# A chunked state-space scan ahead of a gated FFN: the prologue rebuilt around an earlier pair 0

## The chip, the cores and the metric

One core of a Trainium2 chip. The metric is device time of one execution in microseconds (us), the median of the runs. The engines are TensorE (PE; its weight loads are listed apart as PEld), VectorE (DVE), ScalarE (ACT), GpSimd (POOL) and SyncE (SP), which only starts DMAs here.

## The reference

Two parts. First a scan over 768 tokens for 4 batches and 8 heads, in chunks, with head size D = 32 and state size N = 16; then an FFN over all 3072 tokens with 256 features (8 heads x 32).

```python
for c in range(nc):                      # chunks along the sequence
    cum = cumsum(log(a))                 # inside the chunk
    L = exp(cum[i] - cum[j]) * causal
    y_intra = (C @ B.T * L) @ x
    y_inter = C @ state * exp(cum)
    state = exp(sum(la)) * state + (B * exp(cum[-1] - cum)).T @ x
    y[chunk] = y_intra + y_inter
gate = maximum(y @ w_gate, 0)            # y as (3072, 256); w_gate, w_val: 256 x 1536
out = (gate * (y @ w_val)) @ w_out       # w_out: 1536 x 256
```

The result does not depend on the chunk length, and the kernel takes 128 tokens. It also replaces exp(cum[i] - cum[j]) by a product of two factors: with P the running product of a, C is multiplied by P[i] and one of the other factors is divided by P[j].

## The kernel before, in words

**Units.** A *pair* p is 256 tokens of one batch, two chunks of 128 (12 pairs, 3 to a batch). A *block* is 512 tokens, two pairs, the unit of the FFN (6 blocks). In block b the FFN works on pairs 2b and 2b+1 while the scan prepares pairs P = 2b+2 and Q = 2b+3 in between. The scan of pairs 0 and 1 is the prologue. `in_order` (L15) ties every engine to the order of the program, so the order in the code is the order on each engine.

**A pair's steps.** `load` brings x, B and C. `scale_bc` (L253) makes bs in bf16: B divided and C multiplied by the decay P. `cast_x` (L275) casts x. `transp` (L307) turns B and C with TensorE into PSUM, `tevac` (L320) copies them out as BT and, masked for two groups of four heads, as CT. `G` (L355) computes B C^T for all heads into four PSUM banks, `gevac` (L373) copies them to gs and applies the causal mask (ScalarE with POOL for two banks, VectorE with a mask for two). `Dm` (L429) multiplies gs with x into y. `astep` (L393) adds B^T x to the running state in A_ps, `sevac` copies it masked to Sm, `inter` (L417) adds Sm C to y, and `yevac` (L443) copies y to yT, which the FFN reads.

**Wide pairs.** Pairs 0 to 3 (NWIDE = 4) are loaded with two neighbouring tokens on one partition, so that one DMA run is 128 bytes for B and C and 256 for x. Their tokens are therefore not in order on the partitions. `sort_wide` (L286) brings B and x into token order with eight matmuls per pair against a permutation (`order`, L153) and copies the result to bx.

**Decay.** One scan on VectorE gives cp, the running products of each half sequence (L194). Small fp32 matmuls with `pick` bring the wanted heads to the token's partition: `wide_decay` (L201) for a wide pair and `decay` (L227) for all the others, both followed by reciprocals and copies.

**FFN.** `gvh` (L469) is one slice f of 128 hidden units for half a block (256 tokens): four matmuls into one bank, relu on ScalarE to r, product on VectorE to h. `gv` (L455) is the same for 512 tokens and two banks. `fout` (L485) multiplies h with w_out, `foevac` stores the result. A block is four slices as halves (first for pair 2b, then for 2b+1), eight whole ones, then four parts of output, with the scan of P and Q in between.

**Buffers.** PSUM has five shared banks (`bank`, L66) in rotation, for G, gate, val, o and the like, and one each for tp, y and A_ps.

**Start.** `keep_warm` issues matmuls on zeros: 8, then 4 behind the decay matmuls, then 7 after pair 0's G. The weights come in three parts of four slices, and w_out in one, all issued by POOL. `wait_for` (L185) holds POOL's issue of a part until a certain load has landed. The loads of pairs 2 and later are issued by SyncE; B of pair 2 and all that follows it there wait for a memset on VectorE (L81).

Of the kernel before, what the change touches and what calls it, by code (L numbers as in the profile page):

```python
# [29 lines left out]
def kernel(  # L30
# [40 lines left out]

# [3 lines left out]
    def wide_bc(p, qb, qc):  # L75
        b, c0 = p // PPB, 2 * (p % PPB)
        sl = slice(c0 * 128, (c0 + 2) * 128)
        bcr = raw.tile([128, NH, 2, 2, N], FP32, tag="bcr", name="bcr")
        for src, j, q in ((C, 1, qc), (B, 0, qb)):
            if (p, j) in ((0, 0), (2, 1)):  # L80
                nc.vector.memset(bcr[0:1, 0, 0, 0, 0:1], 0.0)  # L81
            q.dma_start(
                out=bcr[:, :, j].rearrange("p h r n -> p h (r n)"),
                in_=src[b, :, sl, :].rearrange("h (p r) n -> p h (r n)", r=2))
        st.setdefault(p, {})["bcr"] = bcr

    def wide_x(p, *qs):

        b, c0 = p // PPB, 2 * (p % PPB)
        sl = slice(c0 * 128, (c0 + 2) * 128)  # L90
        xr = raw.tile([128, NH, 2, D], FP32, tag="xr", name="xr")
        n = NH // len(qs)
        for k, q in enumerate(qs):
            hs = slice(k * n, (k + 1) * n)
            q.dma_start(out=xr[:, hs].rearrange("p h r d -> p h (r d)"),
                        in_=x[b, hs, sl, :].rearrange("h (p r) d -> p h (r d)", r=2))
        st.setdefault(p, {})["xr"] = xr

    def load(p, qx, qb, qc):
        b, c0 = p // PPB, 2 * (p % PPB)  # L100
        if p < NWIDE:
            wide_bc(p, qb, qc)
            wide_x(p, qx)
        else:
            xr = raw.tile([128, 2, NH, D], FP32, tag="xr", name="xr")
            bcr = raw.tile([128, 2, 2, NH, N], FP32, tag="bcr", name="bcr")
            for i in range(2):
                sl = slice((c0 + i) * 128, (c0 + i + 1) * 128)
                qx.dma_start(out=xr[:, i], in_=x[b, :, sl, :].rearrange("h s d -> s h d"))
                for src, j, q in ((B, 0, qb), (C, 1, qc)):  # L110
                    q.dma_start(out=bcr[:, i, j],
                                in_=src[b, :, sl, :].rearrange("h s n -> s h n"))
            st[p] = {"xr": xr, "bcr": bcr}
# [4 lines left out]
    nc.sync.dma_start(out=a_sb, in_=a.rearrange("b h (w s) -> (b h w) s", w=2))  # L118
    first = const.tile([1, 2], FP32)
    nc.vector.memset(first, 0.0)  # L120
    nc.scalar.activation(first[:, 1:2], first[:, 0:1], AF.Relu)


    warm = const.tile([128, 512], BF16)
    nc.vector.memset(warm, 0.0)
    wide_bc(0, nc.scalar, nc.sync)
    wide_x(0, nc.sync, nc.scalar)
    wide_bc(1, nc.scalar, nc.sync)
    wide_x(1, nc.sync)
# [4 lines left out]
    maskUT = const.tile([128, 1, 128], BF16)  # L134
    make_upper_triangular(nc, maskUT[:, 0], 1.0, diag=True)
# [12 lines left out]
    for t in range(2):  # L148
        nc.vector.tensor_scalar_mul(smask[:, t], bd, tmask[:, t:t + 1])
# [3 lines left out]
    order = const.tile([128, 2, 2, 128], BF16)  # L153
    nc.gpsimd.memset(order, 0.0)
    for r in range(2):
        nc.gpsimd.tensor_copy(
            order[:, :, r].rearrange("p c (m r) -> p c m r", r=2)[:, :, :, r],
            ident.rearrange("p (c m) -> p c m", c=2))

    def keep_warm(n):  # L160
        w = bank("w")
        for _ in range(n):
            nc.tensor.matmul(out=w, lhsT=warm[:, 0:128], rhs=warm, start=True, stop=True)  # L163

    keep_warm(8)


# [15 lines left out]
    gate = const.tile([1, 4], FP32)  # L183

    def wait_for(p, j):  # L185

        nc.gpsimd.tensor_copy(gate[:, 2 * j:2 * j + 1], st[p]["bcr"][0:1, 0, j, 0, 0:1])

    wait_for(0, 1)
    weights(0, 4)  # L190

# [9 lines left out]
    def wide_decay(ps):  # L201

        d = bank("wdec", (128, len(ps), 2, 8))
        first = True
        for k, p in enumerate(ps):
            b, c0 = p // PPB, 2 * (p % PPB)
            for i in range(2):
                w, o = (c0 + i) // HC, ((c0 + i) % HC) * 128
                for r in range(2):
                    nc.tensor.matmul(  # L210
                        out=d[64 * i:64 * i + 64, k, r],
                        lhsT=cp[:, o + r:o + 128:2], rhs=pick[:, w, 8 * b:8 * b + 8],
                        start=first or (k == 0 and r == 0), stop=True,
                        tile_position=(0, 64 * i), skip_group_check=True)
                first = False
        return d

    def wide_factors(ps, d):
        f = const.tile([128, len(ps), 2, 2, 8], FP32, name="wf%d" % ps[0])
        nc.vector.reciprocal(f[:, :, 0], d)  # L220
        nc.vector.tensor_copy(f[:, :, 1], d)
        for k, p in enumerate(ps):
            st[p]["f"] = f[:, k].rearrange("p j r h -> p (j r) h")

    scaleBC = glob.tile([128, NB, NC, 2, 8], FP32)

    def decay():  # L227

        d = bank("dec", (128, HC, 2, NB, 8))
        for k in range(HC):  # L230
            nc.tensor.matmul(
                out=d[:, k].rearrange("p w b h -> p (w b h)"),
                lhsT=cp[:, k * 128:(k + 1) * 128],
                rhs=pick.rearrange("p w h -> p (w h)"),
                start=(k == 0), stop=True, skip_group_check=True)
        for w in range(2):
            cs = slice(w * HC, (w + 1) * HC)
            nc.vector.reciprocal(
                scaleBC[:, :, cs, 0, :].rearrange("p b k h -> p k b h"), d[:, :, w])
        for w in range(2):  # L240
            cs = slice(w * HC, (w + 1) * HC)
            nc.scalar.copy(
                out=scaleBC[:, :, cs, 1, :].rearrange("p b k h -> p k b h"), in_=d[:, :, w])

    yT = glob.tile([128, 2, T], BF16)
    A_ps = mm.tile([128, 2, 128], FP32, tag="Aps", name="A_ps")


    def scale(p, eng, ceng):
        scale_bc(p, eng)  # L250
        cast_x(p, ceng)

    def scale_bc(p, eng):  # L253
        b, c0 = p // PPB, 2 * (p % PPB)
        s = st[p]
        bs = att.tile([128, 4, 128], BF16, tag="bs", name="bs")
        if p < NWIDE:
            src = s["bcr"].rearrange("s (t q) j r n -> s (j r) t q n", t=2)
            f = s["f"]
        else:  # L260
            src = s["bcr"].rearrange("s i j (t q) n -> s (i j) t q n", t=2)
            f = scaleBC[:, b, c0:c0 + 2].rearrange("s c j h -> s (c j) h")
        for t in range(2):
            eng.tensor_tensor(  # L264
                out=bs.rearrange("s k (q t n) -> s k t q n", q=4, t=2)[:, :, t],
                in0=src[:, :, t],
                in1=f[:, :, 4 * t:4 * t + 4].to_broadcast([128, 4, 4, N]),
                op=ALU.mult)
        if p < NWIDE:
            s["tin"] = [[bs[:, 2 * j + r] for r in range(2)] for j in range(2)]  # L270
        else:
            s["tin"] = [[bs[:, 2 * i + j] for i in range(2)] for j in range(2)]
            s["B"] = s["tin"][0]

    def cast_x(p, ceng):  # L275
        s = st[p]
        cast = ceng.copy if ceng is nc.scalar else ceng.tensor_copy
        xb = att.tile([128, 2 * NH * D], BF16, tag="xb", name="xb")
        if p < NWIDE:
            cast(xb, s["xr"].rearrange("s h r d -> s (h r d)"))  # L280
            s["xw"] = xb.rearrange("s (h r d) -> s r h d", h=NH, r=2)
        else:
            cast(xb, s["xr"].rearrange("s i h d -> s (i h d)"))
            s["x"] = [xb[:, i * NH * D:(i + 1) * NH * D] for i in range(2)]

    def sort_wide(p, engs=None, own=False):  # L286

        s = st[p]
        bx = att.tile([128, 2, 384], BF16, tag="bx", name="bx")
        for i in range(2):  # L290
            if own and i == 0:
                o = mm.tile([128, 384], FP32, tag="y", name="bxp")
            else:
                o = bank("bxp", (128, 384))
            for r in range(2):
                nc.tensor.matmul(out=o[:, 0:128], lhsT=order[:, i, r], rhs=s["tin"][0][r],
                                 start=(r == 0), stop=(r == 1), skip_group_check=True)
                nc.tensor.matmul(
                    out=o[:, 128:384].rearrange("s (h d) -> s h d", h=NH),
                    lhsT=order[:, i, r], rhs=s["xw"][:, r],  # L300
                    start=False, stop=(r == 1), skip_group_check=True)
            eng = engs[i] if engs else nc.scalar
# [355 lines left out]
```

## Time and profile before

| | |
|---|---|
| median of 3 runs | 133.85 us (132.33, 133.9, 133.85) |
| the profiled execution, first to last instruction | 132.1 us |
| granted TensorE clock | 1.00 throughout |
| busy: TensorE, VectorE, ScalarE, POOL | 125.6, 90.1, 81.7, 37.6 us |
| first FFN tile of block 0 starts | 13.46 us |
| block 1 starts | 37.88 us |
| blocks 2, 3, 4, 5 start | 56.81, 75.43, 93.94, 112.34 us |
| DMA | 12.1 MB in 68995 packets, nearly all under 2 KB |

How to read it: all times are us from the span's start unless marked ns. "out<-in" names the tile written and the tile read. What stands in brackets is idle time of the engine just before, and what ended it. PE is drawn with the modelled ends of its matmuls, which overlap: the distance from start to start tells how fast they run. The page shows the granted clock by slices, DMA by queues, and the chain of waits that ended last.

### The profile page before, as it was taken

To read this page: it belongs to the slowest core of one execution; us is meant where nothing else is said; L and a number is where in the kernel's file an instruction comes from. 1 tells how busy PE (TensorE), PEld (TensorE's weight loads), DVE (VectorE), ACT (ScalarE), POOL (GpSimd) and SP (SyncE) were. 2 spreads that over 40 slices of the span, in tenths; PEclk is the share of its full clock that TensorE was granted. 3 is DMA by queue.
4 is the path that set the end of the run, shared out by engine and by line. 5 is a ranking of instruction groups with operands and counts; after the bars stand their busy time and mean duration, and the time that the engine had idled before them with its cause. 6 is when DMAs were issued, how large, how long until landed. Compare 5 with 4: busy or idle time off the path is not lost.

```text
span 132.1 us, 3133 instructions
## 1 busy us (share of the span) xinstructions
PE 125.6 (95%) x1150; PEld 83.3 (63%) x1157; DVE 90.1 (68%) x196; ACT 81.7 (62%) x177; POOL 37.6 (29%) x76
## 2 busy tenths in 40 slices
PE   6999979999999999999999999999999999999990
PEld 2455655547887457786557785467875577854770
DVE  5648867786478877569977568755879775687511
ACT  4046855393579784488774588744896935876410
POOL 7327374310266000293003390003750022100000
PEclk9999999999999999999999999999999999999999
DMA  3997999996877894239970279761110002200022
GB/s 73 189 183 111 181 210 194 183 144 83 108 136 141 95 118 47 87 86 122 106 83 5 79 137 116 90 64 58 52 57 0 0 0 84 79 0 0 5 88 71
DMA packets 68995, 12.10 MB, mean 92 GB/s; under 512 B 62772, under 2 KB 68980, under 8 KB 68980
## 3 DMA queue, kind: packets, MB, share of 16 engines
q1 hardware_dynamic: 62896, 8.88, 43.7%
q0 software_dynamic: 3184, 2.36, 11.9%
q10 hardware_dynamic: 2896, 0.66, 2.7%
q8 instruction: 9, 0.15, 0.5%
q14 instruction: 10, 0.05, 0.1%
HBM read 11.11 MB, written 3.15 MB: 108 GB/s over the span
## 4 chain that ended last, share of the span: by engine, by line
PE 58%; DVE 1%; issue 0%; DVEq 0%
PE o L490 20%; PE val L463 11%; PE gv L478 11%; PE gate L460 10%; PE y L435 2%; PE g L361 2%; PE A_ps L398 1%; PE tp L318 1%; PE y L424 1%; DVE h L467 0%; DVE ob L503 0%; DVEq L503 0%
## 5 line engine op out<-in xcount | busy, mean ns | idle before, releaser
L467 DVE TENSOR_TENSOR h<-r,val 128x512 bf16<-128x512 bf16 x48 | 32.6, 686 | 9.7 <-ACT r L466 8.8
L490 PE MATMUL o<-wo,h 128*128 128x256 bf16 x288 | 35.0, 273 | 0.1
L466 ACT ACTIVATE r<-gate 128x512 bf16<-128x512 f32 x48 | 28.3, 601 | 8.5 <-PE gate L460 6.2
L369 POOL TENSOR_SCALAR_AFFINE_SELECT gs<-gs 128x512 bf16<-128x512 bf16 (+1 forms) x24 | 12.2, 530 | 65.9 <-ACT gs L380 65.9
L490 PEld LDWEIGHTS <-h 128*128 128x128 bf16 x288 | 27.4, 98 | 5.1 <-issue 1.3
L463 PE MATMUL val<-yT,wv 128*128 128x512 bf16 x96 | 28.6, 379 | 0.3
L460 PE MATMUL gate<-yT,wg 128*128 128x512 bf16 x90 | 27.3, 379 | 0.3 <-ACT r L466 0.3
L482 DVE TENSOR_TENSOR h<-r,gv 128x256 bf16<-128x256 bf16 x48 | 19.9, 421 | 7.3 <-ACT r L481 6.9
L386 DVE TENSOR_TENSOR gs<-g,maskUT 128x512 bf16<-128x512 f32 x24 | 15.5, 686 | 13.0 <-issue 11.8
L481 ACT ACTIVATE r<-gv 128x256 bf16<-128x256 f32 x48 | 18.5, 385 | 2.5 <-PE gv L478 0.9
L478 PE MATMUL gv<-yT,wg 128*128 128x256 bf16 x96 | 18.4, 273 | 0.6 <-ACT yT L448 0.5
L478 PE MATMUL gv<-yT,wv 128*128 128x256 bf16 x96 | 18.3, 273 | 0.0
L463 PEld LDWEIGHTS <-wv 128*128 128x128 bf16 x96 | 9.4, 98 | 11.3
L460 PEld LDWEIGHTS <-wg 128*128 128x128 bf16 x96 | 8.8, 98 | 7.1 <-issue 0.5
L380 ACT CAST gs<-g 128x512 bf16<-128x512 f32 x12 | 7.1, 588 | 9.7 <-PE g L361 9.6
L448 ACT CAST yT<-y 128x512 bf16<-128x512 f32 x12 | 7.0, 586 | 8.2 <-PE y L435 7.1
L478 PEld LDWEIGHTS <-wg 128*128 128x128 bf16 x96 | 9.0, 98 | 2.4 <-issue 1.0
L478 PEld LDWEIGHTS <-wv 128*128 128x128 bf16 x96 | 9.4, 98 | 1.1
L264 POOL TENSOR_TENSOR bs<-bcr,scaleBC 128x256 bf16<-128x256 f32 x16 | 9.6, 623 | 0.0
L506 ACT COPY ob<-o 128x512 f32<-128x512 f32 x10 | 5.9, 586 | 4.7 <-PE o L490 4.7
L163 PE MATMUL w<-warm 128*128 128x512 bf16 x18 | 7.3, 556 | 1.3 <-DVE bcr L81 1.3
L406 DVE TENSOR_TENSOR Sm<-A_ps,smask 128x256 bf16<-128x256 f32 x20 | 8.3, 417 | 0.0
(75 smaller groups left out, 113.1 us busy)
## 6 DMA issues: line engine op xcount, KB each, us to landing
out_dram<-ob SPq DMA_DIRECT2D x10, 256.0 KB, 2.2
xr<-in_x_dram SPq DMA_DIRECT2D x17, 128.0 KB, 3.7
bcr<-in_B_dram SPq DMA_DIRECT2D x16, 64.0 KB, 3.6
bcr<-in_C_dram SPq DMA_DIRECT2D x16, 64.0 KB, 3.3
xr<-in_x_dram SPq DMA_DIRECT2D x3, 256.0 KB, 6.4
wg<-in_moe_w_gate_dram POOLq DMA_DIRECT2D x3, 256.0 KB, 5.0
wv<-in_moe_w_val_dram POOLq DMA_DIRECT2D x3, 256.0 KB, 6.2
wo<-in_moe_w_out_dram POOLq DMA_DIRECT2D x1, 768.0 KB, 11.3
```

The costliest lines, as they stand in the source:

```text
L264: eng.tensor_tensor(out=bs.rearrange("s k (q t n) -> s k t q n", q=4, t=2)[:, :, t], in0=src[:, :, t], in1=f[:, :, 4 * t:4 * t + 4].to_bro ...
L369: nc.gpsimd.affine_select(out=dst, in_=dst, pattern=[[0, n], [1, 128]], compare_op=ALU.is_ge, fill=0.0, base=0, channel_multiplier=-1)
L386: nc.vector.tensor_tensor(out=d[:, q], in0=g[q], in1=m, op=ALU.mult)
L406: nc.vector.tensor_tensor(out=n, in0=A_ps, in1=smask, op=ALU.mult)
L460: nc.tensor.matmul(out=g, lhsT=wg[:, k, fs], rhs=yT[:, k, tk], start=(k == 0), stop=(k == 1))
L463: nc.tensor.matmul(out=v, lhsT=wv[:, k, fs], rhs=yT[:, k, tk], start=(k == 0), stop=(k == 1))
L466: nc.scalar.activation(r, g, AF.Relu)
L467: nc.vector.tensor_tensor(out=fst[b][:, f], in0=r, in1=v, op=ALU.mult)
L478: nc.tensor.matmul(out=gv_[:, j], lhsT=w[:, k, fs], rhs=yT[:, k, tk], start=(k == 0), stop=(k == 1), skip_group_check=True)
L481: nc.scalar.activation(r, gv_[:, 0], AF.Relu)
L482: nc.vector.tensor_tensor(out=fst[b][:, f, u * 256:(u + 1) * 256], in0=r, in1=gv_[:, 1], op=ALU.mult)
L490: nc.tensor.matmul(out=o[:, ts % 2], lhsT=fst[b][:, f, ts * 128:(ts + 1) * 128], rhs=wo[:, f], start=(f == 0), stop=(f == NF - 1), skip_gr ...
```

## The change

It rebuilds what happens before block 0 and in block 0, and how all pairs are scaled.

- **The decay is divided into x, not into B.** `scale_x` makes xb = x / P (one tensor_tensor, 128x512), `cast_b` only casts B, `scale_c` multiplies C by P. In `scale` POOL does all three.
- **Pair 0's C is not scaled at all.** y is multiplied at its evacuation instead, by pb: a row of the decay (cpn) copied by DMA to 32 partitions for each head.
- **x is always loaded in token order** (128-byte runs), also for pairs 0 to 3. B and C of these pairs stay wide. G, inter and yevac use views that undo the order; `causal` gets a second pattern for it.
- **No sorting.** B in token order comes from transposing BT back (`back`, two transposes, and `backevac`).
- **All decay matmuls** run in the prologue, into d0 (pair 0 and C of pair 1) and dall (everything else); ScalarE copies dall to dsb, and `tables` makes the factors from it in block 0.
- **Order.** POOL's waits for loads are gone: eight slices of weights are issued at once. Warm matmuls are 7 and 3 instead of 8, 4 and 7. G(1), back(1) and state(1, 0) stand ahead of the first FFN tile. Loads of pair 2 are held by a memset on VectorE behind state(1, 0), those of pairs 3, 4 and 5 by another in the second half of block 0.
- **Block 0** takes eight slices as halves instead of four. In all blocks `tevac` writes CT with two tensor_scalar instead of one tensor_tensor, and Q's CT is on VectorE instead of ScalarE.

```diff
+    for t in range(2):
+        nc.gpsimd.tensor_tensor(out=smask[:, t], in0=bd, in1=tmask[:, t:t + 1].to_broadcast([128, 128]), op=ALU.mult)
-    keep_warm(8)
+    keep_warm(7)
-    wait_for(0, 1)
     weights(0, 4)
+    weights(4, 8)
...
+    def cast_b(p, eng, j=0):
+        src, dst = views(p, j)
+        for t in range(2):
+            copy(eng, dst[:, :, t], src[:, :, t])
+    def scale_x(p, eng, f=None):
...
+        eng.tensor_tensor(
+            out=xb.rearrange("s (k d) -> s k d", d=D),
+            in0=st[p]["xr"].rearrange("s i h d -> s (i h) d"),
+            in1=f.to_broadcast([128, 2 * NH, D]), op=ALU.mult)
+    def cevac(p, *engs):
...
+        for t in range(2):
+            dst, eng = CT[:, t].rearrange("s i m -> s (i m)"), engs[t % len(engs)]
+            if eng is nc.scalar:
+                eng.mul(dst, src, tmask[:, t:t + 1])
+            else:
+                eng.tensor_scalar_mul(dst, src, tmask[:, t:t + 1])
+    def back(p):
+        s = st[p]
+        s["bt"] = bank("bt", (128, 2, 128), BF16)
+        for i in range(2):
+            nc.tensor.transpose(out=s["bt"][:, i], in_=s["BT"][:, i], identity=ident)
+    def backevac(p, eng):
+        s = st[p]
+        bx = att.tile([128, 2, 128], BF16, tag="bx", name="bx")
+        copy(eng, bx, s.pop("bt"))
+        s["B"] = [bx[:, i] for i in range(2)]
...
     # yevac
+        pb = tokens(p, pb)
+        for t in range(2):
+            eng.tensor_tensor(out=dst[:, t], in0=src[:, t], in1=pb[:, t], op=ALU.mult)
...
     # the prologue: all of the old one is replaced by
+    new_bs(0)
+    cast_b(0, nc.scalar, 0)
+    cast_b(0, nc.scalar, 1)
+    transp(0, 0, True)
+    transp(0, 1, True)
+    cpn = glob.tile([2 * BH, 256], FP32)
+    nc.scalar.mul(cpn, cp[:, 0:256], rmid)
+    pb = glob.tile([128, 2, 256], FP32)
+    for t in range(2):
+        rows = cpn[8 * t:8 * t + 8:2, :]
+        nc.sync.dma_start(out=pb[:, t], in_=rows.unsqueeze(1).to_broadcast([4, 32, 256]))
+    new_x(1)
+    for i in range(2):
+        load_x(1, i, nc.sync)
+    bevac(0, nc.scalar)
+    cevac(0, nc.vector)
+    d0 = mm.tile([128, 6, 8], FP32, tag="Aps", name="d0")
+    dec_token(d0[:, 0:2], 0, True)
+    dec_wide(d0[:, 2:4], 1, False)
+    f0 = const.tile([128, 2 * NH], FP32)
+    nc.vector.reciprocal(f0, d0[:, 0:2].rearrange("p i h -> p (i h)"))
+    nc.vector.tensor_copy(wfac[:, 1], d0[:, 2:4])
     G(0)
+    scale_x(0, nc.vector, f0)
+    back(0)
+    backevac(0, nc.vector)
+    dall = mm.tile([128, HC + 1, 2, NB, 8], FP32, tag="tp", name="dall")
+    dec_all(dall)
+    for p in range(2, NWIDE):
+        dec_wide(dall[:, HC, 0, 2 * (p - 2):2 * (p - 2) + 2], p, False)
     gevac(0, half=False)
...
+    nc.scalar.copy(out=dsb..., in_=dall...)
+    astep(0, 0)
+    keep_warm(3)
+    sevac(0, 0)
+    new_bs(1)
+    cast_b(1, nc.gpsimd)
+    scale_c(1, nc.gpsimd)
+    for w, k, c in ((0, 2, 2), (1, 0, 3)):
+        nc.vector.reciprocal(rfac[:, 0, c], dsb[:, k, w, 0])
+    scale_x(1, nc.gpsimd)
     Dm(0)
     inter(0, 1)
     astep(0, 1)
+    yevac(0, nc.vector, pb)
     sevac(0, 1)
+    transp(1, 1)
+    transp(1, 0)
+    cevac(1, nc.scalar)
+    bevac(1, nc.scalar)
+    G(1)
+    back(1)
+    gevac(1)
+    backevac(1, nc.vector)
+    state(1, 0)
+    nc.vector.memset(st[2]["bcr"][0:1, 0, 1, 0, 0:1], 0.0)
+    load(2, nc.sync)
+    weights(8, NF)
+    weights_out(0, NF)
...
     # block 0: nh = 8 half slices instead of 4; tables() after yevac(W);
     # scale(P) after half slice 2 and the loads of 3, 4, 5 after half slice 4 of the second half,
     # scale(Q) after slice 11, turn(P) after 8, back(P) after 9
```

## Prediction

> **What bounds the kernel now.** I read the page first: TensorE is busy for nearly the whole span.
>
> ```profile
> span 132.1 us, 3133 instructions
> ...
> PE 125.6 (95%) x1150; PEld 83.3 (63%) x1157; DVE 90.1 (68%) x196; ACT 81.7 (62%) x177; POOL 37.6 (29%) x76
> ```
>
> Next the chain of waits in order of time. Its columns are start, length, and what ran.
>
> ```profile
> 56.81 0.87 PE gv L478 x8
> ...
> 75.43 0.87 PE gv L478 x8
> ...
> 93.94 0.87 PE gv L478 x8
> ...
> 112.34 0.87 PE gv L478 x8
> ```
>
> Blocks 2 to 5 start there: 18.6, 18.5 and 18.4 us apart, TensorE alone on the chain. The change leaves their matmuls as they are, so what it is worth shows in when block 1 starts, now 37.88. Then the timeline of the start, for the order on each engine:
>
> ```profile
> 1.29 3.59 PE L163 MATMUL w<-warm 128*128 128x512 bf16 x8 [1.29 <-DVE bcr L81]
> ...
> 8.09 0.69 DVE L352 TENSOR_TENSOR CT<-tp,tmask 128x512 bf16<-128x512 bf16 x1 [1.18 <-PE tp L318]
> ...
> 9.48 0.61 PE L361 MATMUL g<-CT,BT 32*128 32x256 bf16 x8
> ...
> 10.21 1.86 PE L163 MATMUL w<-warm 128*128 128x512 bf16 x6
> ...
> 11.99 0.46 PE L435 MATMUL y<-gs,bx 128*32 128x128 bf16 x16
> ...
> 13.56 0.38 PE L478 MATMUL gv<-yT,wg 128*128 128x256 bf16 x2
> ```
>
> The reader is to see the pair 0 chain: transposes, CT, G, gs, Dm, then the first FFN tile (its weight load at 13.46). Last, block 0 and where TensorE does other work or idles:
>
> ```profile
> 15.13 0.38 PE L478 MATMUL gv<-yT,wg 128*128 128x256 bf16 x2 [0.15 <-DVE h L482]
> ...
> 18.31 0.38 PE L478 MATMUL gv<-yT,wg 128*128 128x256 bf16 x2 [0.47 <-ACT yT L448]
> ...
> 20.14 0.68 PE L210 MATMUL wdec<-pick,cp 64*64 64x8 f32 x16
> ...
> 23.45 0.88 PE L231 MATMUL dec<-pick,cp 64*128 64x64 f32 x6
> ...
> 27.52 0.59 PE L460 MATMUL gate<-yT,wg 128*128 128x512 bf16 x2 [0.28 <-ACT r L466]
> ```
>
> Block 0 takes 37.88 - 13.46 = 24.4 us, 5.8 more than block 2. From start to start in the timeline: G(1) and state between tiles 0 and 1, 13.89 to 15.13: 1.24; the waits for Sm before y, 16.55 to 17.21: 0.66; the wait for yT, 17.66 to 18.31: 0.65; wdec 0.61; dec 0.9; the sort of pair 2 with its wait, 26.25 to 27.52: 1.27; the sort of pair 3: 0.66. Sum 6.0.
>
> **The change, step by step, in us from the span's start.**
>
> *Pair 0 to G.* Its B landed at 4.5 (issued 1.29, 3.2 on the way), its C at 5.5 (1.43, 4.1). No decay is waited for any more. ScalarE casts C in two pieces of 128x128: 128x512 takes 0.59 and 128x256 0.38, so some 0.28 each: 6.1. Two transposes 0.42: 6.6. CT becomes two tensor_scalar of 128x256 on VectorE, not in the trace; bounds 0.27 (256 elements at the 1.04 ns by which rows of 512 and 256 elements differ, nothing fixed) and 0.43 (the smask tensor_scalar of 128x128); I take 0.42, as all other VectorE rows of 128x256 have it: 7.5. G(0) at 7.6 instead of 9.48.
>
> *Pair 0 to Dm.* G 0.61: 8.2; the two transposes of `back` 0.42: 8.6. Then `dec_all` and `dec_wide` of pairs 2 and 3, now ahead of state and Dm: 6 passes like dec (0.88; 1.2 if they run at the early spacing) and 16 like the first wdec (1.05): 10.7. State 0.2, three warm matmuls at 0.43: 12.2. The masks are no longer last: ScalarE's casts end at 9.4, POOL's two selects (1.22) at 10.1; VectorE has f0 0.26, wfac 0.11, xb 0.69, bx 0.42, gs 1.29 from 7.5 on: 10.4. Dm, inter and state 0.8: 13.0, where before stood at 12.67. If the spacing shortens at 10.6 as before, it is 12.0. The scaled evacuation (two of 128x256 on VectorE, 0.85) ends by 13.9 and is hidden by the next step. It needs pb: cpn is written at 6.5, SyncE issues at 6.5 and 7.1, an output store lands after 2.2, contended loads after 5 to 7: 9 to 13, covered in all but the worst. Behind it on SyncE is x of pair 1 (issued 3.21 before, now about 7.7 and 8.3), landing 12.4 to 15 by the same rows; scale_x 1.2 on POOL, needed at 17.
>
> *Pair 1, the price of the change.* G(1), the transposes back and state(1, 0) now stand ahead of the first FFN tile. Transposes 0.43: 13.5; ScalarE does both CT (0.42 each) and BT 0.38 in a row: 14.7; G 0.5: 15.2. The bx copy stands on VectorE behind three gs (1.29 + 0.41) and takes 0.42; TensorE's state matmul waits for it, and the first FFN tile is queued behind that: 17.4, tile at 17.6. Before, tile 1 starts at 15.13, so tile 0 might as well have started at 14.7. Loss 2.9; with the early shortening 1.9 to 2.
>
> *Block 0.* From the first tile to block 1: 16 half pairs of matmuls at 0.433 = 6.93; inter, Dm, state 0.67; four whole tiles 3.47; turn, back, state, inter of pair 2 0.66; output 5.4; G twice 0.66; turn, back of pair 3 0.33; Dm, state 0.45. Sum 18.6, block 2's length by another way. Gone are all 6.0 above.
> But VectorE's queue grows: 16 products of 0.42 + Sm 0.42 + tables (two reciprocals 0.73, copy 0.13) = 8.7 against TensorE's 7.6; then four of 0.69 + CT 0.84 + bx 0.42 + Sm 0.42 = 4.4 against 4.1. It ends 1.4 behind; five banks and the order of the output matmuls take little of it. I take 1.2 (0 to 1.4).
> Sum with short spacing: 17.2 (between 16.6 and 17.6) + 18.6 + 1.2 = 37.0, a gain of 0.9.
>
> *The spacing of matmuls.* Warm matmuls start 0.43 apart until 10.6 and 0.22 after; the granted clock is 1.00 in both. Before, TensorE works with few gaps from 1.29 on. Now it idles from 4.5 to 5.2, runs fp32 matmuls of 8 and 64 columns to 10.7, and idles from 13.5 to 14.7 and 15.6 to 17.4, so the first tiles may run at 0.43. With 3 to 7 us at long spacing (half of it lost) the sum is 17.6 + 18.6 + 2.4 = 38.6, and VectorE's backlog disappears in it: 0.7 lost.
> [...]
>
> *Loads.* `load(2)` is held by a memset behind Sm(1) on VectorE: 18.2, before from 4.48 and 12; `load(3)` about 24. Its x competes with wo (issued 17.9, 11.3 on the way; now about 18.5). x of pair 3 took 11.7 in that place. Pair 2's x may land at 28 to 29.5, +1.2 of scale_x: 30.7 against a state matmul at 28.8: 0 to 1.9, nothing with long spacing.
> The wide x had 256-byte runs, token order has 128. A 256 KB x landed after 6.4 (median), a 128 KB one after 3.7: about the same per byte. [...]
>
> *Later blocks.* Pair Q's CT moves from ScalarE (0.84) to VectorE, which idles 0.97 there for ScalarE in blocks 1 to 3 (the releaser is relu): nothing, at most 0.2 per block either way. POOL's scaling grows from 1.8 to about 2.4 of an engine 29% busy.
>
> **The sum.** 37.0 and 38.6 stand around 37.88; I take no change of the profiled span, 132.1. The shown runs lie 0.23 to 1.8 above that span, the median 1.75. I take 0.9, as which kind the span belongs to is open: 133.0.
>
> **Rivals.** *Faster:* the prologue meets its short side. The earlier G(0) brings the short spacing in time, first tile at 16.3, ScalarE and the banks absorb VectorE's backlog, no late x: 16.3 + 18.6 = 34.9, gain 3.0: 130.0. For it: G(0) starts 1.9 earlier and Dm's operands are ready at 10.4. Against: bx(1) behind gs(1).
> *Slower:* the spacing stays long. If work without gaps from 17.6 needs the same 9.3 us as from 1.29, half is lost: 17.6 + 18.6 + 4.65 = 40.9, loss 3.0: 136.0. It decides from 8.7 us on (2.66 of 133). For it: the idle stretches and the small fp32 matmuls. Against: 2.4 us of dense work after 10.7, and warm matmuls were zeros while tiles aren't. [...]
> *Late x:* the deferred loads cost 1.9 more in the short case, 37.0 + 1.9 = 38.9, the end of block 0 moves 1.0: 134.0. For it the 11.7 of pair 3's x, against it that less is queued before.
> *The covering fails to matter:* eight half tiles leave VectorE as the bound of block 0; that is the 1.2 already in the sum.
>
> **Numbers.** Forecast 40%, late x 10%, faster 27%, slower 23%. What lies around the span is taken alike for both kernels, so the bound of 2%, about what a measurement of this kernel can tell from no change, is 2.7 on the difference of the sums: 3.0 gained or lost lie beyond it, the forecast and the late x inside. That gives 27, 50, 23. Cases of both signs hold half the chance, so the forecast's own range stands here: 131.4 to 134.7 (37.0 less 37.88, with 0.23 around, to 38.6 with 1.8 around). The range reaches down to 129.6 (the faster case with 0.5 around) and up to 136.8 (the slower case with 1.7 around).
>
> **What would show it.** G(0) before 8; first FFN tile between 16.3 and 17.7, its state matmul waiting for VectorE's bx; the spacing of the 16 half tiles, 0.22 or 0.43 per 512 columns; no wdec, dec or order matmuls in block 0; block 1's start against 37.88. Wrong if block 1 starts before 35 or after 40.5, or if blocks 1 to 4 change their length.

## The result, and the profile after

The changed kernel takes 144.7 us (median of 144.92, 144.48, 144.3, 144.92); the kernel before, beside it, 133.12 (132.33, 133.9, 133.85, 132.38). The ratio is 1.088, 95% interval 1.0798 to 1.0962: slower, and 8 us above the upper end of the range (136.8). The profiled execution is one of 144.92 us. Each ratio counts only the executions that lie within 1.5% of the fastest of their kernel, so it can differ from the ratio of the medians.

The page of the changed kernel: TensorE's busy time has hardly grown, the span by 10.8.

```profile
span 142.9 us, 3162 instructions
...
PE 126.5 (89%) x1136; PEld 83.8 (59%) x1136; DVE 91.0 (64%) x214; ACT 76.1 (53%) x172; POOL 45.3 (32%) x101
```

So 10 us of new idle time or stretched work have to be found. Where they lie follows from the block starts in the timeline: the first FFN tile at 19.24 (before 13.56), then blocks 1 to 5 at 43.36, 63.48, 83.44, 103.07 and 122.81. The timeline of the kernel before has them at 37.88, 56.65, 75.26, 93.78 and 112.18 (the table above took the last four from the chain of waits, which has them 0.16 later). Block 1 starts 5.5 late. Blocks 1 to 4 take 20.1, 20.0, 19.6 and 19.7 where they took 18.8, 18.6, 18.5 and 18.4: 5.1 more; block 5, with no pair left to prepare, 0.2 more. Half of the loss is thus in blocks in which the forecast saw none.

The start of the changed kernel in the timeline, to be set against the lines of before that the prediction shows:

```profile
7.31 0.40 PE L360 MATMUL g<-CT,BT 32*128 32x256 bf16 x8
...
12.14 0.62 PE L433 MATMUL y<-gs,xb 128*32 128x128 bf16 x16
...
14.92 0.61 PE L360 MATMUL g<-CT,BT 32*128 32x256 bf16 x8 [1.19 <-ACT BT L261]
15.13 0.44 DVE L459 TENSOR_TENSOR yT<-y,pb 128x256 bf16<-128x256 f32 x1 [3.62 <-DMA pb<-cpn]
...
16.51 0.44 DVE L459 TENSOR_TENSOR yT<-y,pb 128x256 bf16<-128x256 f32 x1 [0.94 <-DMA pb<-cpn]
...
17.56 1.05 POOL L282 TENSOR_TENSOR xb<-xr,rfac 128x512 bf16<-128x512 f32 x1 [6.68 <-DMA xr<-in_x_dram]
...
18.71 0.28 DVE L261 COPY bx<-bt 128x256 bf16<-128x256 bf16 x1
19.05 0.40 PE L393 MATMUL A_ps<-xb,bx 128*128 128x256 bf16 x1 [3.19 <-DVE bx L261]
19.24 0.64 PE L486 MATMUL gv<-yT,wg 128*128 128x256 bf16 x2
```

G(0) and Dm(0) (the y matmuls) are as early as forecast. Then VectorE stands before the y product until the decay products pb land, 3.62 for the first tile and 0.94 for the second. Everything behind it in its queue shifts with it: gs of pair 1, its bx copy, and TensorE's state matmul with the first FFN tile behind. What holds the tile here is one chain through two engines' queues, started by a DMA that the forecast had "covered". A second limit stands close behind it: POOL gets x of pair 1 only at 17.56, and the state matmul that reads the scaled x could not have started before 18.61.

Block 2 of the changed kernel around the turn of pair P, and the last two lines at that of Q:

```profile
70.37 0.60 DVE L328 TENSOR_SCALAR CT<-tp,tmask 128x256 bf16<-128x256 bf16 x2
...
71.06 0.37 ACT L261 COPY BT<-tp 128x256 bf16<-128x256 bf16 x1 [1.33 <-PE gate L469]
...
71.33 1.58 ACT L475 ACTIVATE r<-gate 128x512 bf16<-128x512 f32 x3
...
71.96 1.28 DVE L476 TENSOR_TENSOR h<-r,val 128x512 bf16<-128x512 bf16 x2 [0.99 <-ACT r L475]
...
74.79 0.37 ACT L261 COPY BT<-tp 128x256 bf16<-128x256 bf16 x1 [1.88 <-PE val L472]
...
75.71 0.59 PE L472 MATMUL val<-yT,wv 128*128 128x512 bf16 x2 [0.51 <-ACT r L475]
```

The same place in the kernel before:

```profile
62.96 0.37 ACT L338 COPY BT<-tp 128x256 bf16<-128x256 bf16 x1
...
63.39 0.60 ACT L466 ACTIVATE r<-gate 128x512 bf16<-128x512 f32 x1
63.54 0.68 DVE L352 TENSOR_TENSOR CT<-tp,tmask 128x512 bf16<-128x512 bf16 x1
```

Before, ScalarE copies BT first and VectorE's CT follows. After, CT comes first and BT starts 0.09 behind its end. The row names TensorE's gate matmul, the last event that ended before it, but BT reads nothing of that, and the transposes that it does read ran at 69.36. ScalarE stood still for 1.33, the relu of the FFN is queued behind BT, three of them then run in a row, and VectorE waits 0.99 for the first. At the turn of Q the same wait, 1.88, reaches TensorE: its next val matmul stands 0.51 until a relu has run. By the tile's own view, ScalarE idled ahead of BT in all eight of its copies of blocks 1 to 4:

```profile
L261 ACT COPY BT<-tp x8: 372/372/373, 51.8 to 114.3; 128x256 bf16<-128x256 bf16 x8
...
its engine sat idle before it (us, times) until:
  PE val L472: 5.6, 3
  PE gate L469: 5.3, 4
  DVE CT L328: 1.9, 1
```

That is 12.8 us of ScalarE's queue standing in front of a copy. The new `tevac` has the two calls in the other order, `cevac` before `bevac`, and both copies read the one PSUM tile `tp`. Neither writes what the other reads; still BT, written later, starts 0.09 behind CT's end here, and in e3 below the list of waits puts 13.0 us of eight such copies down to CT. Why BT waits, and what would happen without the wait, no run here shows.

### The profile page after: what moved, and what is told of

Read it like the earlier page. It is cut to its first block, busy times and chain, and to the rows that moved or that the text cites. A ratio compares the mean times of both kernels' runs of the same rounds, so it can differ in the third digit from the quotient of the medians.

```text
span 142.9 us, 3162 instructions
## 1 busy us (share of the span) xinstructions
PE 126.5 (89%) x1136; PEld 83.8 (59%) x1136; DVE 91.0 (64%) x214; ACT 76.1 (53%) x172; POOL 45.3 (32%) x101
## 5 line engine op out<-in xcount | busy, mean ns | idle before, releaser
L476 DVE TENSOR_TENSOR h<-r,val 128x512 bf16<-128x512 bf16 x44 | 29.5, 685 | 12.9 <-ACT r L475 11.8
L143 POOL TENSOR_SCALAR_AFFINE_SELECT gs<-gs 128x512 bf16<-128x512 bf16 (+1 forms) x24 | 12.4, 537 | 61.2 <-ACT gs L373 61.2
L490 DVE TENSOR_TENSOR h<-r,gv 128x256 bf16<-128x256 bf16 x56 | 22.9, 419 | 7.9 <-ACT r L489 7.4
L475 ACT ACTIVATE r<-gate 128x512 bf16<-128x512 f32 x44 | 24.7, 603 | 4.7 <-PE gate L469 4.4
L489 ACT ACTIVATE r<-gv 128x256 bf16<-128x256 f32 x56 | 21.4, 384 | 7.6 <-PE gv L486 5.2
L379 DVE TENSOR_TENSOR gs<-g,masks 128x512 bf16<-128x512 f32 x24 | 15.4, 685 | 12.3 <-issue 9.5
L486 PE MATMUL gv<-yT,wg 128*128 128x256 bf16 x112 | 22.7, 286 | 0.0
L486 PE MATMUL gv<-yT,wv 128*128 128x256 bf16 x112 | 22.5, 285 | 0.0
L282 POOL TENSOR_TENSOR xb<-xr,rfac 128x512 bf16<-128x512 f32 x11 | 11.5, 1047 | 12.9 <-DMA xr<-in_x_dram 7.8
L261 ACT COPY BT<-tp 128x256 bf16<-128x256 bf16 x11 | 4.1, 372 | 15.2 <-PE val L472 5.6
L261 ACT CAST yT<-y 128x512 bf16<-128x512 f32 (+1 forms) x14 | 7.0, 527 | 7.7 <-PE y L433 7.5
```

The source lines that it names most:

```text
L143: nc.gpsimd.affine_select(out=dst, in_=dst, pattern=pattern, compare_op=ALU.is_ge, fill=0.0, base=0, channel_multiplier=-1)
L261: (eng.copy if eng is nc.scalar else eng.tensor_copy)(out=out, in_=in_)
L282: eng.tensor_tensor(out=xb.rearrange("s (k d) -> s k d", d=D), in0=st[p]["xr"].rearrange("s i h d -> s (i h) d"), in1=f.to_broadcast([128, ...
L379: nc.vector.tensor_tensor(out=d[:, q], in0=g[q], in1=m, op=ALU.mult)
L475: nc.scalar.activation(r, g, AF.Relu)
L476: nc.vector.tensor_tensor(out=fst[b][:, f], in0=r, in1=v, op=ALU.mult)
```

## The experiments

Theory A: the order of the two copies in `tevac` makes ScalarE wait, and this is what lengthens blocks 1 to 4. Theory C: the rest is the order of the DMAs, pb and the late x of pair 1. Rivals: CT of pair Q on VectorE is itself the burden; G(1) with its evacuations ahead of the first tile sets the start whatever the DMAs do; the long spacing of matmuls.

**e1: the order of the copies.**
```diff
     def tevac(p, beng, *cengs):
-        cevac(p, *cengs)
         bevac(p, beng)
+        cevac(p, *cengs)
```


> The changed kernel with one swap: after a turn the copy of BT on ScalarE is issued before that of CT on VectorE, from pair 2 on. In the changed kernel's trace ScalarE idles 1.33 us before BT until VectorE has written CT (70.37 to 70.97), and the relu of the next slice stands behind BT; blocks 1 to 4 are 20.1, 20.0, 19.6 and 19.8 us long against 18.9, 18.6, 18.5 and 18.4. Theory A, that order makes ScalarE's queue wait for VectorE's: blocks 1 to 4 go back to 18.4 to 18.9, 5.2 us in all, and block 0, with two such turns, gives 1 to 2 more: 137.5 to 139. Rival B, Q's CT on VectorE is simply too much work for VectorE: blocks 1 to 4 stay within 0.3 of 20, 144 to 144.7.

Measured: 137.02 us (before 132.58), ratio 1.0299 (1.0235 to 1.0364): 7.7 us less than the changed kernel. Blocks 1 to 4 take 18.5, 18.5, 18.5 and 18.4, as before the change, with CT of pair Q still on VectorE. Block 1 starts at 41.41, not 43.36. ScalarE's idle time ahead of BT in the same view:

```profile
L261 ACT COPY BT<-tp x8: 372/372/373, 48.6 to 106.1; 128x256 bf16<-128x256 bf16 x8
its engine sat idle before it (us, times) until:
  issue: 0.8, 4
```

12.8 has become 0.8. Theory A stands (its gain is even a little larger than expected), and the burden of CT on VectorE is excluded.

**e2: the second half of the first weights later.**
```diff
-    weights(4, 8)          # behind weights(0, 4)
...
     gevac(0, half=False)
+    weights(4, 8)
```


> The changed kernel with the second part of the weights (slices 4 to 7) issued by POOL after pair 0's causal selects, at about 9.7 us instead of 4.9. In the changed kernel pb is issued at 6.6 and VectorE waits for it until 15.1 and 16.5, x of pair 1 lands at 17.5, while four weight loads are on the way. Theory C, these weights hold pb and x back: pb lands by 12 to 13, the first FFN tile starts at 16.5 to 17.7 instead of 19.24, time 143 to 143.4. Rival D, pb is slow by itself (one partition read 32 times): pb still lands after 14.5 and the time stays at 144.3 to 144.9.

Measured: 145.8, ratio 1.0977 (1.0892 to 1.1062), no gain. pb is in time now (y products at 13.89), but x of pair 1, behind pb on SyncE, now travels with the late weights: POOL's scaling at 19.90, first tile at 21.17. With pb issued at 6.4 and 7.1, both transfers took less than 7.5. Theory C is right on pb and too simple on what follows: with one transfer early, another is the last.

**e3: the same order put into the kernel before** (pairs 2 and on; CT of pair Q to VectorE with it).
```diff
-        (beng.copy if beng is nc.scalar else beng.tensor_copy)(rows(BT), tokens(0))
+        if p < 2:
+            (beng.copy if beng is nc.scalar else beng.tensor_copy)(rows(BT), tokens(0))
...
+        if p >= 2:
+            (beng.copy if beng is nc.scalar else beng.tensor_copy)(rows(BT), tokens(0))
...
-                tevac(Q, nc.scalar, nc.scalar)
+                tevac(Q, nc.scalar, nc.vector)
```


> The kernel before with two edits that the change made in the later blocks: from pair 2 on CT is issued before BT, and Q's CT is on VectorE. Nothing else. Theory A: blocks 1 to 4 become 1.1 to 1.4 longer each, block 0 a little, 133 goes to 138 to 140. Rival E, the later blocks are longer for another reason (order of loads, scaling on POOL, longer queue of x): no more than 1 us over the kernel before.

Measured: 139.42, ratio 1.0502 (1.0411 to 1.0593), 6.8 us slower than before. Its blocks 1 to 4 take 20.2, 20.0, 19.7 and 19.8, the changed kernel's lengths, with the old prologue. In its list of waits from 40 to 140 (total, times, longest) the wait bears its name:

```profile
ACT BT L356 <- DVE CT L353: 13.0, 8, 1.9
```

The two runs give the order nearly the same price from both sides, 6.8 put in and 7.7 taken out. The edit here had to move pair Q's CT as well, since before both of Q's copies ran on ScalarE; by e1 that move costs nothing by itself.

**e4: e1 and e2 together.**


> The changed kernel with the swap of BT and CT and the second part of the weights late. If both theories hold and are independent, 136 to 138, that is the sum of the two gains; if the late first tile was hidden by stalls of block 0 that the swap removes, the second gain is less than 0.5 beside the swap.

Measured: 138.04, ratio 1.039 (1.0322 to 1.0457); first tile at 20.45, block 1 at 42.19. The late weights gain nothing here either: e1 alone took 137.02 with block 1 at 41.41, and in e4, as in e2, x of pair 1 is what comes last (POOL's scaling at 19.18).

**e5: e4 with x of pair 1 ahead of pb** (only what e4 hasn't is shown).
```diff
+    new_x(1)               # behind C1 on SyncE
+    for i in range(2):
+        load_x(1, i, nc.sync)
...
-    new_x(1)               # behind pb
```


> The changed kernel with B's copy ahead of C's in the loop's tevac, weights 4 to 7 issued behind the evacuation of G(0), and the two loads of pair 1's x issued on SyncE right behind B1 and C1, ahead of the decay products. Theory (order of the DMAs holds the first FFN tile): x of pair 1 lands at 10 to 11 instead of 17.5 to 19.8, the decay products at 10 to 13, the first FFN tile comes at 16.0 to 17.7 instead of 19.3 (with the order of the copies alone) or 20.5 (with the weights late alone), block 1 starts at 39.0 to 39.5, time 134.5 to 136. Rival (G(1), its evacuations and the state matmul ahead of the first tile set it, whatever the DMAs do): first tile not before 18.5, time 136.5 to 138.

Measured: 138.9, ratio 1.0463 (1.0355 to 1.0571), a miss: the first tile came at 21.62, later than in e4. x arrives in time (POOL scales it at 13.23), and pb is late instead:

```profile
6.67 4.96 SPq L531 DMA_DIRECT2D pb<-cpn  x2
...
15.57 0.45 DVE L461 TENSOR_TENSOR yT<-y,pb 128x256 bf16<-128x256 f32 x1 [3.10 <-DMA pb<-cpn]
...
18.90 0.45 DVE L461 TENSOR_TENSOR yT<-y,pb 128x256 bf16<-128x256 f32 x1 [2.88 <-DMA pb<-cpn]
```

SyncE needs 4.96 to hand over two pb transfers behind the x loads, where it needed 1.32 in the changed kernel. In each of the orders of e1, e2 and e5 at least one of the two is late.

**e6: e5 with the load of pair 2 right behind `sevac(0, 0)`.**


> The run before it plus the load of pair 2 (B, C, x) issued right behind the evacuation of the first state, ahead of G(1). Theory (pair 2's x came 1.5 us late in block 0): the wait of the state matmul of pair 2 for the scaled x goes away, 0.5 to 1.5 us less than the run before it. Rival: the load competes with the first weights and with the decay products, first tile later by as much, no gain.

Measured: 138.44, ratio 1.0399 (1.0313 to 1.0486); block 1 at 43.05, the same as in e5. The wait that this load was to end had gone in e5 already (TensorE stood 0.24 ahead of that state matmul, with the tiles so much later), so the run tells only that the earlier load costs nothing that shows.

**e7: e6 with 12 warm matmuls of 256 columns behind `back(1)`.**


> The run before it plus 12 matmuls of 256 columns, whose result nobody reads, put on TensorE behind back(1), where it waits for the first FFN tile. Theory (the first tiles of block 0 run at the long spacing, about 0.43 per 512 columns, since TensorE idled ahead of them): first tiles at 0.22, 1.5 to 2.5 us less than the run before it. Rival: 12 matmuls (2.6 to 3.0 us) are too few, or the spacing follows something else: spacing as before, and 0 to 1 us more where they stand ahead of the first tile.

Measured: 138.32, ratio 1.0403 (1.0307 to 1.05). The 12 ran at the long spacing from 15.42 on (2.54 us), TensorE idled 2.95 behind them, and the first four tiles ran at 0.43 per step as before. No gain; too few, or too early.

**e8: e6 with G(1), its evacuations, state(1, 0) and the later weights behind the first FFN tile.**


> The second run of this group (load of pair 2 early) with G(1), its evacuations and the state matmul of pair 1, with the weights 8 and on and the output weights, issued behind the first FFN tile instead of ahead of it. Theory (pair 1's block ahead of the first tile costs what stands between the y products and the first tile): first tile 0.4 to 1.5 us earlier, time less by as much. Rival: TensorE's idle there is the wait for the decay products or the first weights, and the block only moves: time the same within 0.4 us.

Measured: 139.66, ratio 1.0467 (1.0355 to 1.0578), no gain; block 1 of the profiled execution (140.9) starts at 45.19. The two matmuls of the tile's gate half now wait for pb one by one:

```profile
17.59 0.37 PE L488 MATMUL gv<-yT,wg 128*128 128x256 bf16 x1 [2.85 <-DVE yT L461]
20.12 0.37 PE L488 MATMUL gv<-yT,wg 128*128 128x256 bf16 x1 [2.17 <-DVE yT L461]
```

**e9: e1 with pb made by TensorE.** `sel` is a 0/1 matrix of which row of the products belongs to which partition.
```diff
-        nc.sync.dma_start(out=pb[:, t], in_=rows...)
...
-    keep_warm(3)
+    for t in range(2):
+        nc.tensor.matmul(out=pbp[:, t], lhsT=sel[:, t], rhs=cpn, ...)
+    nc.scalar.copy(out=pb, in_=pbp)
```


> The changed kernel with B's copy ahead of C's in tevac, and the decay products of pair 0 brought to the token partitions by two f32 matmuls against a 0/1 matrix and a copy by ScalarE, in place of the two DMAs from SBUF to SBUF and of the three warm matmuls; the loads of pair 1's x are then no longer behind these DMAs on SyncE. Theory (these two DMAs, 8.5 us each on the way and ahead of x on SyncE, hold the first FFN tile): the y products start at 14.0 to 14.6 instead of 15.2 and 16.6, x of pair 1 lands before 13, the first FFN tile comes at 16.5 to 18.8 instead of 19.3 (with the order of the copies alone), block 1 starts at 39.0 to 40.8, time 134.5 to 136.5. Rival (G(1) with its evacuations ahead of the tile sets it anyway): first tile at 18.5 to 19.5 and time 136.5 to 137.5.

Measured: 136.67 (before 132.86), ratio 1.0253 (1.0172 to 1.0335). pb is no longer waited for, and the first tile is as late as ever:

```profile
14.54 0.78 DVE L465 TENSOR_TENSOR yT<-y,pb 128x256 bf16<-128x256 f32 x2 [2.46 <-PE y L428]
...
18.51 0.28 DVE L267 COPY bx<-bt 128x256 bf16<-128x256 bf16 x1
...
18.85 0.40 PE L399 MATMUL A_ps<-xb,bx 128*128 128x256 bf16 x1 [1.64 <-DVE bx L267]
19.04 0.64 PE L492 MATMUL gv<-yT,wg 128*128 128x256 bf16 x2
```

The rival holds here: G(1), gs and bx ahead of the tile take up the 4.5 us from the y products on. So e8 removed one of two limits, e9 the other, and each left the whole tile at 19 to 20. The two stand on different runs (e8 on e6, where SyncE handed pb over later; e9 on e1); pair 1 behind the tile on e1 alone was not run.

**e10: e9 with pair 1 behind the tiles.**
```diff
-    G(1); back(1); gevac(1); backevac(1); state(1, 0)
...
             gvh(b, f, 0)
+            if b == 0 and f == 0:
+                G(1); back(1); gevac(1); backevac(1); weights(8, NF); ...
+            if b == 0 and f == 2:
+                state(1, 0)
```


> The run before it with G(1), its evacuations and the weights 8 and on behind the first FFN tile, and the state matmul of pair 1 behind the third; the load of pair 2 then no longer waits for them. Theory (with the products there in time, pair 1's block is what stands ahead of the first tile): first tile at 14.9 to 16.0, no wait for the x of pair 2, block 1 starts at 37.0 to 39.0, time 131.5 to 134.0. Rival (the tile finds no weights, or the long matmul spacing of the first tiles eats it): first tile as expected, but block 1 not before 39.5, time 135 to 137.

Measured: 133.32 (131.43 to 134.59, 10 runs) beside 132.86, ratio 0.9992 (0.9931 to 1.0053): the whole loss is gone.

```profile
13.71 0.78 DVE L465 TENSOR_TENSOR yT<-y,pb 128x256 bf16<-128x256 f32 x2 [2.46 <-PE y L428]
14.21 0.70 PE L492 MATMUL gv<-yT,wg 128*128 128x256 bf16 x2
...
14.82 1.05 POOL L288 TENSOR_TENSOR xb<-xr,rfac 128x512 bf16<-128x512 f32 x1 [3.92 <-DVE bcr L581]
```

First tile at 14.21, 4.8 earlier than in e9, block 1 at 37.85 (before 37.88). The gain from e9 to e10 (3.4 in the start of block 1) is one that neither e8 nor e9 could show alone. Not all of it is the order of pair 1: the edit also lets pair 2's load start at 14.8 instead of 19.8, and TensorE stands 0.23 instead of 0.95 ahead of that pair's first state matmul.

**e11: e10 with the decay matmuls behind the second tile**, and pair 1's own decays by four narrow matmuls ahead of G(0).


> The run before it (e10) with the decay matmuls of all chunks and their copy issued behind the second FFN tile instead of ahead of Dm(0), and the decays of pair 1's x by four narrow matmuls ahead of G(0) in their place. Theory (on this path the early decay matmuls, 2.6 us, stand between G(0) and pair 0's y): first FFN tile at 11.5 to 12.5 instead of 14.2, block 1 starts at 36.5 to 37.5 instead of 37.9, time 131.0 to 132.8. Rival (the weights, issued at 3.3 to 4.9, or the long spacing of the first tiles take the place): first tile not before 13.5, or block 1 not before 37.7, time within 0.4 of the run before it.

Measured: median 135.37 over 13 runs (131.82 to 135.67) beside 133.34, ratio 0.9914 (0.9838 to 0.999). The first tile came at 12.60, but block 1 at 38.59: the decay matmuls (2.45 us) only changed places, from ahead of the first tile to between the second and third. The ratio rests on two of the 13 executions, and the median is 2.0 above that of before, so this is not shown to beat either kernel.

**e12: e11 with TensorE's gaps at 4.4 to 6.1 filled** (8 warm matmuls for 7, and 3 between the transposes of pair 0).


> The run before it (e11) with 8 instead of 7 warm matmuls at the start and 3 more between the transposes of pair 0's B and C, where TensorE stood still for 0.5 and 1.1 us. Theory (these gaps, at 4.4 to 6.1, are why the matmuls from 7.7 to about 21 run at the long spacing): the spacing stays short behind 7.7, first FFN tiles at 0.22 per 256 columns and weight pair instead of 0.43, block 1 starts at 35.5 to 37, time 129.5 to 131.5. Rival (the f32 decay matmuls of 8 and 64 columns, which keep the array nearly empty, or something else sets the spacing): spacing long from about 7.7 to 15 or later as before, time as e11 or up to 0.5 above it.

Measured: median 134.53 over 12 runs (132.06 to 135.04) beside 132.97, ratio 0.9993 (0.9916 to 1.007; it rests on three of the 12). The long spacing only began later: the matmuls that make pb took 1.13 instead of e11's 2.07, and the one behind the state matmul at 9.74 followed after 0.22, but the tiles from 12.19 to 23.7 ran at 0.43. The gaps are not the cause, or not the only one.

## Why the prediction was wrong

**Right:** *Pair 0 to G* (7.6 forecast, 7.31 measured) and, within 0.3, *Pair 0 to Dm* (12.0 to 13.0 for its end; the y matmuls and state end by 13.3). CT's pieces took 0.30 each, nearer to the lower bound 0.27 than to the 0.42 taken. *Block 0* was sized well for what it described: in e1, with the copies in order, it takes 41.41 - 19.31 = 22.1, which is 18.6 + 1.7 for four tiles at long spacing + 1.5 for the late x of pair 2, and a rest of 0.3 that holds whatever came of the 1.2 put down to VectorE. *The late x of pair 2* (0 to 1.9) was 1.5 there, though "nothing with long spacing" was said of it and the spacing was long: its load was issued 1.8 later than forecast (20.0 for 18.2). *The price of the order of pair 1*, 2.9, is some 2.7 in e9 and e10 (3.4 in the start of block 1, less the 0.7 that pair 2's earlier load saved). *The spacing* was long for the first tiles: 19.05 to about 24.5, some 5.4 us, of which half is 2.7 against the 2.4 forecast. Nothing in the run of before shows the 3 to 7 us at long spacing that the sum took for it, an estimate of the author's; measured were these 5.4, and 3.4 in e1.

**The step that failed:** *Later blocks*, "nothing, at most 0.2 per block either way". It asked on which engine pair Q's CT runs and what idle time covers it, and did not ask in which order `tevac` issues it. What the runs showed in its place: ScalarE's BT copy waits for VectorE's CT, 12.8 us in eight copies. By e3 and e1 that order costs 6.8 to 7.7 us, 1.1 to 1.6 of it in each of blocks 1 to 4, and in the changed kernel 2 ahead of block 1. The forecast's own test, "if blocks 1 to 4 change their length", names it, and its other one, block 1 after 40.5, was met too (43.36). "The change leaves their matmuls as they are, so what it is worth shows in when block 1 starts" was the premise for it: the matmuls are the same, but ScalarE's relu, for which they wait in turn (val by 0.51 at 75.71), was set behind a wait.

**Terms of the sum that were mis-sized:** *pb* "9 to 13, covered in all but the worst" landed at 15.1 and 16.5, 8.5 and 9.2 after its issue. The bound of 5 to 7 was too narrow by the kernel before itself, where a load of B took up to 10.0 and the x of pair 3 the 11.7 that the forecast names elsewhere; "in all but the worst" was the case that came, and what is queued behind the waiting product on VectorE (Sm, gs and bx of pair 1, hence the state matmul and the tile) had not been named. *x of pair 1* "12.4 to 15, needed at 17" was there at 17.56: SyncE held its second load until 13.4. The first tile came at 19.24 instead of 17.6.

**The miss as a sum,** from the forecast's case with long spacing (block 1 at 38.6) to the measured span: 1.6 by the first tile, 3.1 in block 0 (2.0 of it the order of the copies, by e1), 5.1 in blocks 1 to 4 and 0.2 in block 5.

**The rivals:** *Slower* gave 136.0 by the long spacing; the sign came true and the mechanism did not. The long spacing ended 3.4 us after the state matmul ahead of the first tile in e1 (19.13 to 22.5) and 5.4 after it in the changed kernel, not 9.3. One length for all runs is not shown: it was 9.3 us at the start of the kernel before (1.29 to 10.6), and 13.6 in e10 (below).

## What to carry to other kernels

When two engines read one PSUM tile, look in the built program which waits for which, and let the engine whose queue carries the critical work (here ScalarE with the relus) be the one that goes first; the order of two lines was worth 6.8 to 7.7 us of 133. "Covered" is a claim about everything queued behind the waiting instruction, on its engine and on the next, not about that instruction. And where two limits stand side by side, undoing either alone shows nothing (e8, e9): undo both before calling a part harmless.

## What the runs showed of the hardware

A small transfer from SBUF to SBUF, 128 KB that repeats four rows 32 times, took 8.5 and 9.2 us in the changed kernel, until the product that waited for it started, while weights were loading (1.05 MB in their queue from 6.5 to 16.6). In e2, with half of these weights later, it was less than 7.5; in e10 two f32 matmuls against a 0/1 matrix and a copy did the same in 2.07 + 0.59 us.

The granted clock in the records is 0.50 from 7.6 to 24.5 in the changed kernel and from 7.6 to 21.2 in e10, and the matmuls run at the long spacing there. But e5's record says 1.00 from 7.6 to 24.5, and its first tiles, from 21.62 on, ran at 0.43 all the same; so did the warm matmuls of the changed kernel from 1.26 on, under 1.00. A record of 1.00 does not prove the short spacing. In e10 the long stretch lasted 13.6 us with TensorE busy for nearly all of it:

```profile
7.60:14.20 6.60, 6.49 (x52) 4.74 (x51) 3.09 (x9) 1.93 (x4) 2.54 (x6) 0.50 1.33 201
14.20:21.20 7.00, 6.60 (x51) 3.70 (x50) 4.42 (x13) 3.85 (x11) 5.00 (x8) 0.50 0.68 97
```

The columns are the stretch, its length, the busy time of TensorE, its weight loads, VectorE, ScalarE and POOL, the granted clock, the DMA share and GB/s: 13.09 us busy of 13.6, at half clock. What starts and ends such a stretch stays open; e12 shows only that filling the early gaps moves its start, to about 10. Transposes of B and C into two PSUM banks in place of the shared `tp`, which might make the order of the copies harmless, were not tried.
